# Attention and routed feed-forward on one Trainium2 core: the products with v in one piece for each half of the queries

## The chip, the cores and the metric

The kernel runs on one core of a Trainium2 chip. The metric is the device time of one execution in microseconds (us), from the launch to the end. Five engines work side by side, each through its own list of instructions in order: PE (TensorE: matrix products and transposes; the profile lists its weight loads apart, as PEld), DVE (VectorE), ACT (ScalarE), POOL (GpSimd) and SP (SyncE, which here only issues DMAs). PE writes into PSUM, which is divided into banks; DVE and ACT read PSUM and write the result to SBUF. An instruction that needs another engine's result waits on a semaphore, and everything behind it on its own engine waits too.

## The reference

Attention over 8 batches, 8 heads, 576 positions and head size 64, with a position bias from a small network, then a top-1 mixture of 8 experts over the 4608 tokens. Cut to what matters:

```python
scores = scale * np.matmul(q, k.transpose(0, 1, 3, 2))
scores = scores + bias.transpose(2, 0, 1)[None, :, :, :]
scores = scores - np.max(scores, axis=-1, keepdims=True)
attn = np.exp(scores)
attn = attn / (np.sum(attn, axis=-1, keepdims=True) + 1e-09)
attn_out = np.matmul(attn, v)
...
e_idx = np.argmax(logits, axis=1)
for e in range(E):
    mask = e_idx == e
    h = np.maximum(x[mask] @ w1[e], 0.0)
    out[mask] = gate_w[mask, None] * (h @ w2[e])
```

## The kernel before

Three stages follow each other: a table of the position bias, the attention (with the routing of finished batches spread through it), and the expert tiles. The change lies in the attention, `attention()` at L584. It runs over 32 pairs of heads (8 batches of 4 pairs) and one more turn that finishes the last pair. A turn n has five units u = 0 to 4. What a unit does, and in which order, is a string of letters in the table `ORDER` (L576 to L582); `attention()` walks through the letters and emits the instructions of each step. No scheduler moves anything afterwards, so the order of the letters is the order on every engine.

The letters that matter here:

- `S` is `scores()` (L415): the products of q and k for one slot (128 queries of one head; nine slots a pair, numbered S0 to S8 in this text, the last with six products instead of four) on PE into the PSUM tile `sps0` or `sps1`, then one DVE operation (L445) that adds the bias and finds the minimum (the score is kept negated).
- `e` and `f` are `exps()` (L457): the exponential of the unit's first and second slot on ACT.
- `T` and `t` are `etrans()` (L466) for part 1 and part 0: four transposes of a block of the exponentials on PE, into the PSUM tile `eps1` or `eps0`, and a copy into `eT` on ACT or DVE. The blocks are numbered by query chunk and part: e31 is chunk 3 part 1. Units 2, 3 and 4 do chunks 0, 1 and 2 of the turn's own pair; units 0 and 1 do chunks 3 and 4 of the pair before. Chunk 4 has only 64 queries for each head; its part 0 is e40 (L479, in `t` of unit 1), and its part 1 is the narrow one, e41 (L484, in `T` of unit 1), written into 64 columns of the array at a time.
- `R` is `rtrans()` (L495): four transposes of the last 64 keys of each row, copied into `rT` by ACT.
- `a A` and `b c` are `av()` (L504) of the pair before: the products of v and `eT`. Each half of the queries (288) takes eight of them, four key chunks for two heads, each in 64 columns of the array (L517), and one 128-wide product with the last 64 keys (L527), all summed in one PSUM bank. In the kernel before, a half comes in two pieces: `a` and `b` do key chunks 0 and 1, `A` and `c` do chunks 2 and 3, the 128-wide product, and the copy to `xT` on ACT (called av0 and av1).
- digits are `prep()` (L368): transposes of q and k of the next pair. `X` and `B` are steps of the routing, where there are any. `W`, `K`, `V`, `L` issue DMAs from SP; `C`, `q`, `k` are copies on POOL.

The PSUM banks `xps0` and `xps1` are handed out in turn by `xbank()` (L306): to `R`, the digits, `av()` and `X`. Which engine copies a block out of PSUM stands in `ON_ACT` (L310):

```python
ON_ACT = ("av0", "av1", "e00", "e11", "e20", "e30", "e31", "e40", "e41", "prep2", "prep5", "rT", "xr")
```

So e31, e30 and e40 are all copied by ACT, in this order, and e30 and e40 go through the same PSUM tile, `eps0`.

Of the kernel before, what the change touches and what calls it, by code (L numbers as in the profile page):

```python
# [22 lines left out]
S = 576  # L23
D = 64
# [4 lines left out]
HS = S // 2  # L29
# [78 lines left out]
class Attn:  # L108
# [392 lines left out]
            nc.tensor.transpose(ps[:, P * c : P * c + P], rem.rearrange("p h w -> p (h w)"), self.idf)  # L501
        self.take("rT", self.rT[:, 0:512], ps)

    def av(self, n, half, part):  # L504

        nc = self.nc
        if half == 0 and part == 0:
            self.xT[n] = self.xTb[n // NP % 2][:, n % NP, :]
        if part == 0:
            self.avps = self.xbank()  # L510
        v = self.vmain[n]
        sl = slice(HS * half, HS * half + HS)
        ps = self.avps[:, 0:HS]
        for k in (0, 1) if part == 0 else (2, 3):
            for h in range(2):
                o = slice(64 * h, 64 * h + 64)
                nc.tensor.matmul(  # L517
                    ps[o, :],
                    v[:, h, k, :],
                    self.eT[:, h, k, sl],  # L520
                    start=k == 0,
                    stop=False,
                    tile_position=(0, 64 * h),
                    skip_group_check=True,
                )
        if part == 1:
            nc.tensor.matmul(ps, self.vrem[n % 2], self.rT[:, sl], start=False, stop=True, skip_group_check=True)  # L527
        if part == 1:
            self.take(f"av{half}", self.xT[n][:, sl], ps)
            if half == 1:  # L530
                del self.vmain[n]

    def first_steps(self, route):

# [39 lines left out]


    ORDER = (  # L576
# [5 lines left out]
    )  # L582

    def attention(self):  # L584
        n_pair = self.n_pair
        tail = self.first_tiles() if self.K else {}
        for at in self.ROUTE_LATE:
            tail.setdefault(at, []).append(lambda: next(self.route, None))
        for u, k in self.LATE:
            tail.setdefault((0, u), []).append(lambda k=k: next(self.late[k], None))  # L590
        bg = None
        for n in range(n_pair + 1):
            for u in range(5):
                for f in tail.get((n, u), ()):
                    f()
                if u == 4 and n > 0 and n % NP == 0:
                    assert not bg or all(k == len(x) for x, k in bg)
                    bg = self.route_steps(n // NP - 1)
                m, w = (n, u - 2) if u >= 2 else (n - 1, u + 3)
                scored = []  # L600
                for op in self.ORDER[u].split():
                    if op in "SefC":
                        if n == n_pair:
                            continue
                        if op == "S":
                            scored.append(self.scores(n, 2 * u + len(scored)))
                        elif op == "C":
                            self.compact(n, u)
                        else:
                            self.exps(*scored["ef".index(op)])  # L610
                    elif op in "tT":
                        if 0 <= m < n_pair:
                            self.etrans(m, w, "tT".index(op))
                    elif op in "RaAbc":
                        if n > 0:
                            self.rtrans(n - 1) if op == "R" else self.av(n - 1, *divmod("aAbc".index(op), 2))
                    elif op in "01234WKV":
                        if n + 1 < n_pair:
                            if op in "01234":
                                self.prep(n + 1, int(op))()  # L620
                            else:
                                {"W": lambda: self.swap(n + 1), "K": lambda: self.heads(n + 1), "V": lambda: self.load_v(n + 1)}[op]()
                    elif op in "qkL":
                        if n + 2 < n_pair:
                            self.load_qk(n + 2) if op == "L" else self.split(n + 2, "qk".index(op))
                    elif op == "D":
                        self.route_store()
                    elif op == "Z":
                        self.route_scatter()
                    elif f := self.route_next(bg, "XB".index(op)):  # L630
                        f()
                if 0 <= m < n_pair:
                    del self.E[m, w]
        while self.scatters:
            self.route_scatter()
        self.bg = bg
# [836 lines left out]
```

## Time and profile before

| | |
|---|---|
| median of 3 runs | 1158.28 us (1153.8 to 1158.3) |
| the profiled execution's own time | 1160.33 us |
| its span, first to last instruction | 1158.4 us |
| mean granted TensorE clock | 0.99 of full speed |
| DVE, ACT, POOL busy, of the span | 65%, 63%, 31% |
| one pair in the middle of the attention, transposes of `R` to those of the next | 18.5 to 19.1 us |
| attention, first to last product with v | 86 to 679 us |

The profile is a trace of one execution. A row of the timeline gives the start in us, the length, the engine, the line of the kernel, the operation, what it writes and reads, the shape, how many instructions are merged into the row and, in brackets, how long the engine stood idle before it and what ended that. Each source-level product in full precision shows as two or more instructions, and a PE row overlaps the next by the depth of the array, so distances between starts are the safer measure. In all, 1024 instructions belong to L517 and 128 to L527.

### The profile page before, as it was taken

Reading aid. Unit: us, or ns where it says so; the run is one execution under the profiler, and the core shown is the slowest. Engines: PE = TensorE matmul, PEld = TensorE weight load, DVE = VectorE, ACT = ScalarE, POOL = GpSimd, SP = SyncE. Lnnn points to the kernel's source line nnn. Section 1 sums busy time; section 2 is a strip of 40 time slices with the busy share of each in tenths; the row PEclk is TensorE's granted clock in tenths of the full one; section 3 lists DMA queues with packets and bytes.
Section 4 is the critical chain, followed back from the end, with each engine's and each line's share of the span. In section 5 each row is a group of like instructions: output and inputs, shape, how many; then the busy total and the mean of one; then the engine's idle time right before and its main releaser. Section 6 shows DMA issues by size and latency. Waiting matters only on the chain. (4 is left out here: it accounts for less than half of the span.)

```text
span 1158.4 us, 23054 instructions
## 1 busy us (share of the span) xinstructions
PE 1121.5 (97%) x8202; PEld 912.4 (79%) x8202; DVE 748.6 (65%) x1556; ACT 731.8 (63%) x1420; POOL 361.0 (31%) x514
## 2 busy tenths in 40 slices
PE   7989999999999999999999999999999999999997
PEld 3457877778777777877777769899999999999975
DVE  8965667676675766756668547584566455645576
ACT  7776767767676676776766646454555455545576
POOL 0013334435434444254352234412112222212122
PEclk9989999999999999999999989999999999999999
DMA  6984434635545544454463721211115115112370
GB/s 176 222 173 113 107 97 124 115 96 130 110 108 121 123 122 104 105 129 108 121 121 96 204 33 56 60 47 46 56 38 175 62 57 196 42 47 65 110 261 26
DMA packets 91456, 124.54 MB, mean 108 GB/s; under 512 B 35713, under 2 KB 60673, under 8 KB 91332
## 3 DMA queue, kind: packets, MB, share of 16 engines
q1 hardware_dynamic: 83236, 101.61, 34.8%
q0 software_dynamic: 8000, 21.35, 6.2%
q8 instruction: 68, 1.11, 0.5%
q14 instruction: 56, 0.46, 0.2%
q10 hardware_dynamic: 96, 0.00, 0.0%
HBM read 140.36 MB, written 19.90 MB: 138 GB/s over the span
## 5 line engine op out<-in xcount | busy, mean ns | idle before, releaser
L445 DVE CUSTOM_DVE_ANT_0 Eb<-sps,NBm 128x576 f32<-128x576 f32 x256 | 189.6, 754 | 160.0 <-PE sps L430 89.1
L459 ACT ACTIVATE Eb<-Eb,mn 128x576 f32<-128x576 f32 x288 | 221.4, 769 | 36.9 <-DVE mn L445 33.5
L430 PE MATMUL sps<-KT,QT 128*128 128x288 f32 x1152 | 220.4, 317 | 3.9 <-DMA QT<-QT 3.7
L430 PEld LDWEIGHTS sps<-KT,QT 128*128 128x128 f32 x1152 | 164.6, 190 | 9.0 <-issue 4.5
L1188 PE MATMUL p<-QT,w1hi 128*128 128x256 f32 x1152 | 162.2, 284 | 0.0
L473 PE MATMUL eps<-idf,Eb 128*128 128x128 f32 x1024 | 158.5, 281 | 0.6 <-DVE lgs L810 0.3
L517 PE MATMUL xps<-eT,vraw 128*64 128x288 f32 x1024 | 155.1, 425 | 1.5 <-DVE QT L1173 1.0
L1188 PEld LDWEIGHTS p<-QT,w1hi 128*128 128x128 f32 x1152 | 149.5, 192 | 2.2 <-ACT w1hi L1161 0.8
L473 PEld LDWEIGHTS eps<-idf,Eb 128*128 128x128 f32 x1024 | 113.9, 141 | 39.0 <-issue 29.3
L1191 DVE SCALAR_TENSOR_TENSOR hl<-p,hh 128x512 fp32r<-128x512 f32 x72 | 49.7, 690 | 141.5 <-ACT hh L1190 140.0
L1214 POOL DMA_INDIRECT out<-mo,idt x36 | 48.0, 1333 | 298.5 <-ACT mo L1213 262.4
L464 POOL COPY rem<-Eb 128x128 f32<-128x128 f32 x128 | 37.2, 291 | 318.8 <-ACT Eb L459 312.3
L1155 DVE TENSOR_TENSOR w2lo<-NBm,w2hi 128x1024 fp32r<-128x1024 f32 x84 | 102.3, 1224 | 24.8 <-ACT w2hi L1154 18.7
L1205 PE MATMUL p<-w2hi,hh 128*128 128x512 f32 x288 | 115.3, 400 | 0.0
L315 ACT ACTIVATE eT<-eps 128x512 f32<-128x512 f32 x192 | 110.6, 591 | 6.8 <-PE eps L473 5.9
L1205 PE MATMUL p<-w2hi,hl 128*128 128x512 f32 x288 | 113.7, 395 | 0.0
L1190 ACT ACTIVATE hh<-p 128x512 fp32r<-128x512 f32 x72 | 43.0, 597 | 111.5 <-PE p L1188 101.3
L315 ACT ACTIVATE xTb<-xps 128x288 f32<-128x288 f32 x64 | 26.3, 411 | 117.0 <-PE xps L527 114.4
L517 PEld LDWEIGHTS xps<-eT,vraw 128*64 128x64 f32 x1024 | 63.2, 138 | 46.1 <-issue 12.3
L1155 DVE TENSOR_TENSOR w1lo<-NBm,w1hi 128x1024 fp32r<-128x1024 f32 x84 | 97.7, 1225 | 0.2 <-ACT w1hi L1154 0.2
L1188 PE MATMUL p<-QT,w1lo 128*128 128x256 f32 x576 | 92.9, 284 | 1.0 <-DVE w1lo L1162 1.0
L1154 ACT CAST w2hi<-NBm 128x1024 fp32r<-128x1024 f32 x84 | 86.8, 1040 | 0.7 <-PEq L1318 0.7
(235 smaller groups left out, 1945.9 us busy)
## 6 DMA issues: line engine op xcount, KB each, us to landing
NBm<-moe_w SPq DMA_DIRECT2D x24, 2048.0 KB
NBm<-moe_w SPq DMA_DIRECT2D x46, 1024.0 KB
QT<-QT SPq DMA_DIRECT2D x64, 304.0 KB
NBm<-xTb SPq DMA_DIRECT2D x32, 288.0 KB
KH<-KT SPq DMA_DIRECT2D x64, 144.0 KB
qraw<-q SPq DMA_DIRECT2D x32, 256.0 KB
kraw<-k SPq DMA_DIRECT2D x32, 256.0 KB
vraw<-v SPq DMA_DIRECT2D x32, 256.0 KB
```

The costliest lines, as they stand in the source:

```text
L315: self.nc.scalar.activation(out, ps, AF.Copy, scale=scale)
L430: nc.tensor.matmul(ps[:, half, :], q, k[:, HS * half : HS * half + HS], start=i == 0, stop=i == len(terms) - 1, skip_group_check=True,)
L445: nc.vector.tensor_tensor_reduce(out=e.rearrange("p (t w) -> p t w", t=2), in0=ps, in1=nb.rearrange("p (t w) -> p t w", t=2), scale=1.0, s ...
L459: self.nc.scalar.activation(e, e, AF.Exp, bias=mn, scale=-1.0, accum_out=sm)
L473: nc.tensor.transpose(ps[:, k, :], e[:, part, P * k : P * k + P], self.idf)
L517: nc.tensor.matmul(ps[o, :], v[:, h, k, :], self.eT[:, h, k, sl], start=k == 0, stop=False, tile_position=(0, 64 * h), skip_group_check=True,)
L1154: self.nc.scalar.copy(h, w)
L1155: self.nc.vector.tensor_tensor(l, w, h.bitcast(F32), op=ALU.subtract)
L1188: nc.tensor.matmul(ps[:, a, :], w[:, c, fs], x[:, c, :], start=i == 0, stop=i == len(ops) - 1)
L1191: nc.vector.scalar_tensor_tensor(hl[:, sl, :], ps, 0.0, hh[:, sl, :].bitcast(F32), op0=ALU.max, op1=ALU.subtract)
L1205: nc.tensor.matmul(ps, h[:, f, sl], m[:, f, :], start=i == 0, stop=i == len(ops) - 1)
L1214: nc.gpsimd.indirect_dma_start(out=self.out, out_offset=IndirectOffsetOnAxis(ap=ids, axis=0), in_=o, in_offset=None, bounds_check=self.n_t ...
```

## The change

`av()` loses its argument `part`: one call does all eight products of a half, the 128-wide product and the copy. The table `ORDER` has one letter for each half instead of two. `a` (first half) stands in unit 1 behind `T`, the narrow transposes, instead of `a` in unit 0 and `A` in unit 1. `b` (second half) stands where it stood, in unit 2, and takes in what `c` did in unit 3. In unit 1 `T` moves up from the end to a place ahead of `a`, and `0` comes behind `a`; in unit 0 `t` directly follows `T`.

```diff
-    def av(self, n, half, part):
+    def av(self, n, half):
...
-        if part == 0:
-            self.avps = self.xbank()
...
-        ps = self.avps[:, 0:HS]
-        for k in (0, 1) if part == 0 else (2, 3):
+        ps = self.xbank()[:, 0:HS]
+        for k in range(4):
...
-        if part == 1:
-            nc.tensor.matmul(ps, self.vrem[n % 2], self.rT[:, sl], start=False, stop=True, skip_group_check=True)
-        if part == 1:
-            self.take(f"av{half}", self.xT[n][:, sl], ps)
-            if half == 1:
-                del self.vmain[n]
+        nc.tensor.matmul(ps, self.vrem[n % 2], self.rT[:, sl], start=False, stop=True, skip_group_check=True)
+        self.take(f"av{half}", self.xT[n][:, sl], ps)
+        if half == 1:
+            del self.vmain[n]
...
     ORDER = (
-        "S R S e f X T a t B C Z",
-        "L D S 1 A t e S 4 f 0 C T",
+        "S R S e f X T t B C Z",
+        "L D S 1 t e S 4 f T a 0 C",
         "t S W S e f b q C Z T",
-        "B S c e S T 3 2 t f C V",
+        "B S e S T 3 2 t f C V",
         "S K k X X e T B X t D",
     )
```

The lines of `av()` are L515 and L524 in the changed kernel. The first place is PE's list in units 0 and 1, from e31 (`eps1`) to e40 (L479 into `eps0`). Before, in turn 10:

```order
L473 MATMUL eps1_739<-idf_62,Eb_88 128x128 [waits DVE_49,Activation_49]
L473 MATMUL eps1_739<-idf_62,Eb_88 128x128 x3
L517 MATMUL xps1_78<-eT_103,vraw9_2588 64x288 [waits DMAHW7_49,Activation_49]
L517 MATMUL xps1_78<-eT_103,vraw9_2588 64x288 x3
L473 MATMUL eps0_738<-idf_62,Eb_88 128x128 x4
L430 MATMUL sps0_736<-KT0_107,QT0_72 128x288 [waits DVE_49]
L430 MATMUL sps0_736<-KT0_107,QT0_72 128x288 x3
L379 MATMUL xps0_77<-idr_102,qs_105 128x128 [waits Activation_49]
L379 MATMUL xps0_77<-idr_102,qs_105 128x128 x3
L517 MATMUL xps1_78<-eT_103,vraw9_2588 64x288 x4
L527 MATMUL xps1_78<-rT_104,vrem1_116 128x288 [waits DMAHW1_49,DMAHW0_49]
L479 MATMUL eps0_738<-idf_62,Eb_88 128x128 [waits Activation_49]
```

The same stretch of PE's list in the changed kernel, in the same turn, again from e31 to e40:

```order
L473 MATMUL eps1_739<-idf_62,Eb_88 128x128 [waits DVE_49,Activation_49]
L473 MATMUL eps1_739<-idf_62,Eb_88 128x128 x3
L473 MATMUL eps0_738<-idf_62,Eb_88 128x128 [waits Activation_49]
L473 MATMUL eps0_738<-idf_62,Eb_88 128x128 x3
L430 MATMUL sps0_736<-KT0_107,QT0_72 128x288 [waits DVE_49]
L430 MATMUL sps0_736<-KT0_107,QT0_72 128x288 x3
L379 MATMUL xps1_78<-idr_102,qs_105 128x128 x4
L479 MATMUL eps0_738<-idf_62,Eb_88 128x128 [waits Activation_49]
L479 MATMUL eps0_738<-idf_62,Eb_88 128x128 x3
```

Both pieces of the first half have left the stretch between e31 and e40; between the two uses of `eps0` there remain one group of scores and one of prep. In both kernels the first transpose of e40 waits on ACT.

The second place is PE's list from the second scores of unit 2 (`sps1`) to the second of unit 3, with the second half of the products with v. Before:

```order
L430 MATMUL sps1_737<-KT0_107,QT0_72 128x288 [waits DVE_49]
L430 MATMUL sps1_737<-KT0_107,QT0_72 128x288 x3
L517 MATMUL xps1_78<-eT_103,vraw9_2588 64x288 [waits Activation_49]
L517 MATMUL xps1_78<-eT_103,vraw9_2588 64x288 x3
L473 MATMUL eps1_739<-idf_62,Eb_88 128x128 [waits Activation_49]
L473 MATMUL eps1_739<-idf_62,Eb_88 128x128 x3
L430 MATMUL sps0_736<-KT0_107,QT0_72 128x288 [waits DVE_49]
L430 MATMUL sps0_736<-KT0_107,QT0_72 128x288 x3
L517 MATMUL xps1_78<-eT_103,vraw9_2588 64x288 x4
L527 MATMUL xps1_78<-rT_104,vrem1_116 128x288
L430 MATMUL sps1_737<-KT0_107,QT0_72 128x288 [waits DVE_49]
L430 MATMUL sps1_737<-KT0_107,QT0_72 128x288 x3
```

The changed kernel's PE list over the same stretch, which here begins with both scores of unit 2:

```order
L430 MATMUL sps0_736<-KT0_107,QT0_72 128x288 x4
L430 MATMUL sps1_737<-KT0_107,QT0_72 128x288 x4
L515 MATMUL xps1_78<-eT_103,vraw9_2588 64x288 [waits Activation_49]
L515 MATMUL xps1_78<-eT_103,vraw9_2588 64x288 x7
L524 MATMUL xps1_78<-rT_104,vrem1_116 128x288
L473 MATMUL eps1_739<-idf_62,Eb_88 128x128 x4
L430 MATMUL sps0_736<-KT0_107,QT0_72 128x288 [waits DVE_49]
L430 MATMUL sps0_736<-KT0_107,QT0_72 128x288 x3
L430 MATMUL sps1_737<-KT0_107,QT0_72 128x288 [waits DVE_49]
L430 MATMUL sps1_737<-KT0_107,QT0_72 128x288 x3
```

The eight products stand together, and the two groups of scores of unit 3 now follow each other with nothing between.

The third place is ACT's list in units 0 and 1: from the exponential of S1 (`mn10_1`) over the copies of e31 (`eps1`), e30 (`eps0`), av0 (`xTb`) and e40 (`eps0`) to the exponential of S2. Before:

```order
L459 ACTIVATE Eb_88,sums10_2852<-Eb_88,mn10_1_2864 128x576 [waits DVE_49,Activation_49]
L315 ACTIVATE eT_103<-eps1_739 128x4x128 [waits PE_49]
L315 ACTIVATE eT_103<-eps0_738 128x4x128 [waits PE_49]
L315 ACTIVATE xTb0_94<-xps1_78 128x288 [waits PE_49]
L315 ACTIVATE eT_103<-eps0_738 128x4x2x64 [waits PE_49]
L459 ACTIVATE Eb_88,sums10_2852<-Eb_88,mn10_2_2906 128x576 [waits DVE_49]
```

ACT's list in the changed kernel over the same stretch, continued to av0:

```order
L459 ACTIVATE Eb_88,sums10_2852<-Eb_88,mn10_1_2864 128x576 [waits DVE_49,Activation_49]
L315 ACTIVATE eT_103<-eps1_739 128x4x128 [waits PE_49]
L315 ACTIVATE eT_103<-eps0_738 128x4x128 [waits PE_49]
L315 ACTIVATE eT_103<-eps0_738 128x4x2x64 [waits PE_49]
L459 ACTIVATE Eb_88,sums10_2852<-Eb_88,mn10_2_2902 128x576 [waits DVE_49]
L315 ACTIVATE KT1_108<-xps0_77 128x2x64 [waits DMAHW4_49,DMAHW2_49,DVE_49]
L459 ACTIVATE Eb_88,sums10_2852<-Eb_88,mn10_3_2919 128x576 [waits Activation_49]
L315 ACTIVATE rT_104<-eps1_739 128x64 [waits PE_49]
L315 ACTIVATE xTb0_94<-xps1_78 128x288 [waits PE_49]
```

On ACT only av0 has moved, behind the copy of e41 (`rT`); the copies of e31 and e30 still stand behind the exponential of S1.

More of the change, by code (lines that the diff above doesn't have):

```diff
@@ L502, in rtrans @@
         self.take("rT", self.rT[:, 0:512], ps)
-    def av(self, n, half, part):
+    def av(self, n, half):
         nc = self.nc
-        if half == 0 and part == 0:
+        if half == 0:
             self.xT[n] = self.xTb[n // NP % 2][:, n % NP, :]
-        if part == 0:
-            self.avps = self.xbank()
         v = self.vmain[n]
         sl = slice(HS * half, HS * half + HS)
-        ps = self.avps[:, 0:HS]
-        for k in (0, 1) if part == 0 else (2, 3):
+        ps = self.xbank()[:, 0:HS]
+        for k in range(4):
             for h in range(2):
@@ L613, in attention @@
                             self.etrans(m, w, "tT".index(op))
-                    elif op in "RaAbc":
+                    elif op in "Rab":
                         if n > 0:
-                            self.rtrans(n - 1) if op == "R" else self.av(n - 1, *divmod("aAbc".index(op), 2))
+                            self.rtrans(n - 1) if op == "R" else self.av(n - 1, "ab".index(op))
                     elif op in "01234WKV":
```

## The prediction

> **What bounds the kernel now.** I read the page first, then the waits of PE in the middle of the attention (200 to 588 us), then the timeline of single pairs. The page says who is busy:
>
> ```profile
> PE 1121.5 (97%) x8202; PEld 912.4 (79%) x8202; DVE 748.6 (65%) x1556; ACT 731.8 (63%) x1420; POOL 361.0 (31%) x514
> ```
>
> PE is busy 97% of the span, and no other engine passes 65%. An average can hide stages, so the waits of PE inside the attention come next (who waited for whom, us in total, times, longest):
>
> ```profile
> PE xps L866 <- DVE base L847: 1.5, 5, 0.3
> PE xps L771 <- DVE xrb L317: 1.1, 3, 0.4
> PE sps L430 <- DMA QT<-QT: 0.4, 1, 0.4
> ```
>
> That is the whole list: 3.0 us in 388. PE is the bound there, and each microsecond taken from or added to its list moves the end by as much. That holds only as long as the other engines deliver in time, and how near they are must be read from the order. Units 0 and 1 of a turn, on PE, from e31 (514.03) by `a`, e30, S2, prep 1, `A` and its 128-wide product to e40 (L479):
>
> ```profile
> 514.03 0.60 PE L473 MATMUL eps<-idf,Eb 128*128 128x128 f32 x4
> 514.56 1.19 PE L517 MATMUL xps<-eT,vraw 128*64 128x288 f32 x8
> 515.68 0.66 PE L473 MATMUL eps<-idf,Eb 128*128 128x128 f32 x4
> 516.09 0.78 PE L430 MATMUL sps<-KT,QT 128*128 128x288 f32 x4
> 516.71 0.45 PE L379 MATMUL xps<-idr,qs 128*128 128x128 f32 x4
> 517.09 1.19 PE L517 MATMUL xps<-eT,vraw 128*64 128x288 f32 x8
> 518.21 0.75 PE L527 MATMUL xps<-rT,vrem 128*128 128x288 f32 x2
> 518.80 0.60 PE L479 MATMUL eps<-idf,Eb 128*128 128x128 f32 x4
> ```
>
> ACT at the same time: the exponential of S1, then the copies of e31 and e30 in one row of two, with no idle time in brackets:
>
> ```profile
> 515.09 0.78 ACT L459 ACTIVATE Eb<-Eb,mn 128x576 f32<-128x576 f32 x1
> ...
> 515.86 1.11 ACT L315 ACTIVATE eT<-eps 128x512 f32<-128x512 f32 x2
> ```
>
> The copy of e30 ends at 515.86 + 1.11 = 516.97. e40 needs the same PSUM tile and starts at 518.80, 1.83 us later. So ACT, though busy 63%, is only 1.83 us ahead here, and what keeps it ahead is PE's work on `a` and `A`.
>
> **The change: what PE saves.** Every entry into the 64-column products and every way out of them costs PE time. The way out, in the weight loads:
>
> ```profile
> 515.68 0.42 PEld L473 LDWEIGHTS eps<-idf,Eb 128*128 128x128 f32 x4 [0.44 <-issue]
> ```
>
> The next weights are not loaded beside the running products, as elsewhere, but 0.44 us later. To price whole pieces I use distances between starts, with these rows of units 1 to 4 of the pair before:
>
> ```profile
> 501.51 0.22 PE L384 MATMUL xps<-idr,qs 128*128 128x128 f32 x1
> ...
> 502.07 0.34 PE L484 MATMUL eps<-idf,Eb 128*64 128x64 f32 x4
> 502.33 0.66 PE L473 MATMUL eps<-idf,Eb 128*128 128x128 f32 x4
> 502.74 1.30 PE L430 MATMUL sps<-KT,QT 128*128 128x288 f32 x8
> 503.98 1.19 PE L517 MATMUL xps<-eT,vraw 128*64 128x288 f32 x8
> 505.10 0.66 PE L473 MATMUL eps<-idf,Eb 128*128 128x128 f32 x4
> 505.51 0.78 PE L430 MATMUL sps<-KT,QT 128*128 128x288 f32 x4
> ...
> 508.46 0.60 PE L473 MATMUL eps<-idf,Eb 128*128 128x128 f32 x4
> 508.81 0.88 PE L379 MATMUL xps<-idr,ks 128*128 128x128 f32 x8
> 509.53 0.63 PE L473 MATMUL eps<-idf,Eb 128*128 128x128 f32 x4
> ...
> 511.66 1.04 PE L473 MATMUL eps<-idf,Eb 128*128 128x128 f32 x8
> ```
>
> - Unit prices. Four transposes ahead of another group take 0.35 (508.46 to 508.81), and ahead of more transposes 0.44 (eight in 1.04, the last of them about 0.27 long, so 0.11 each). Four of prep take 0.36 (eight from 508.81 to 509.53). A piece of four products with v and the way out takes 1.12 (503.98 to 505.10). Its row of 1.19 has four steps of two concurrent products; a product is 0.41 long, so a step is at most 0.26, and the first is slower, so I take 0.245. Eight products then take 1.12 + 4 x 0.245 = 2.10. The 128-wide product takes 0.59 (518.21 to 518.80).
> - Units 0 and 1, e31 to e40: 518.80 - 514.03 = 4.77 before. Left are e31 0.44, e30 0.35, S2 0.62 (516.09 to 516.71) and prep 1 0.36, together 1.77. PE's list is shorter by **3.00**.
> - Unit 3: from S6 (505.51) to e11 (508.46) 2.95. Two groups of scores take 1.24 up to a product with v (502.74 to 503.98), and 0.09 of that is the entry (514.03 to 514.56 is 0.53 where four transposes take 0.44), so 1.15 is left: shorter by **1.80**.
> - Unit 1, from prep 4 to S4: 501.51 to 502.74 is 1.23 before, with prep 0. Now prep 4 0.20, the narrow transposes 0.26 (502.07 to 502.33), eight products 2.10, the 128-wide one 0.59, prep 0 0.36, e00 0.35, together 3.86: longer by **2.63**.
> - Unit 2, `b` and the transposes behind it: 503.98 to 505.51 is 1.53; now 2.10 + 0.59 + 0.35 = 3.04: longer by **1.51**.
>
> The sum is -3.00 - 1.80 + 2.63 + 1.51 = -0.66, say 0.7 us a pair, 32 x 0.7 = **22 us** less work in PE's list. DVE, ACT, POOL and the DMAs have as many instructions as before.
>
> **The change: what PE now waits for.** The 3.00 us that leave units 0 and 1 were the cover of ACT. The copy of e30 cannot come sooner: it stands behind the exponential of S1, which needs DVE's operation on S1, which needs S1 on PE, and none of these moved ahead. So e40 reaches PE's head 3.00 us sooner against a copy that had 1.83 us in hand: a wait of 3.00 - 1.83 = 1.17 us. This pair is the good end. The bad end is a pair whose routing steps delay DVE, two pairs later:
>
> ```profile
> 554.18 1.05 ACT L315 ACTIVATE eT<-eps 128x512 f32<-128x512 f32 x2
> ...
> 556.30 0.49 PE L479 MATMUL eps<-idf,Eb 128*128 128x128 f32 x3
> ```
>
> Here the hand is 556.30 - 555.23 = 1.07, the wait 1.93. With the middle, 1.55, over the 31 turns that have both a pair before and scores of their own: **48 us**. Behind e40 on PE stand S3, prep 4, the narrow transposes, `a` and prep 0; DVE and ACT wait for these in turn, with no work to fill the time.
>
> Smaller places. SP passes nothing new, but prep 0 comes later behind `a`, so the swap `W` is issued later; it is first needed by S0 of the next turn, some 8 us on, and PE's waits on that transfer were 0.4 us in all. `a` takes its bank from prep 1, whose DVE copy stands before DVE's operation on S3; with PE held at e40 that copy is early. In unit 3 S6 and S7 now come back to back, so DVE's copy of e01 and its operations on S6 and S7 queue:
>
> ```profile
> 506.47 0.75 DVE L445 CUSTOM_DVE_ANT_0 Eb<-sps,NBm 128x576 f32<-128x576 f32 x1
> ...
> 508.66 0.76 DVE L445 CUSTOM_DVE_ANT_0 Eb<-sps,NBm 128x576 f32<-128x576 f32 x1 [1.43 <-PE sps L430]
> ```
>
> They stood 2.19 us apart. ACT's chain from there to e30 (exponentials of S6, S7, S8, S0, S1 with the copies between) can fall behind PE by between nothing (it had idle time in the stretch) and about 0.4 us; I take 0.15, **5 us** in all, and keep 0 and 12 for the range.
>
> **The clock.** A longer idle time of PE can cost more than itself. Windows of the trace (length, PE busy, PEclk, DMA):
>
> ```profile
> 664.73:668.14 3.41, 1.66 (x12) 1.00 0.01 0
> 668.14:674.97 6.83, 6.23 (x25) 0.50 0.73 88
> 1108.35:1111.77 3.42, 2.25 (x10) 1.00 0.43 146
> ```
>
> After 3.41 us with 1.66 busy (1.75 idle) the granted clock is 0.50; a window with 1.17 idle (1108.35), which holds a wait as long as the good end here, drew nothing: the mean clock of the whole span is 0.99. The waits of 1.2 to 1.9 us straddle that boundary. Where one falls whole into such a window, 3.41 us at half clock cost another 1.7 us. I count half of the 8 pairs at the bad end: 4 x 1.7 = **7 us**.
>
> The Trainium skill (TensorE: Matmul & The Clock Gate, "Why this matters for your kernels") says that only idle gaps of over about 3 us between bursts bring the clock down. By that rule no wait here would, and the sum would be 7 us less. The trace does not agree: the row above shows half clock behind 1.75 us of idle time.
>
> **The sum.** On the profiled execution's own 1160.3 us (its span is 1158.4): 1160.3 - 22 + 48 + 5 + 7 = 1198. That execution lies 2 us above the median of the runs, 1158.3, so 1196.
>
> **Rivals.**
> - *The saving comes alone* (8%): the copy of e30 is no bound, and PE has 22 us less to do: 1136. For it speaks that ACT and DVE are idle over a third of the time. It decides where the copy of e30 ends within 1.77 us of e31's start, or the wait stays under 0.7 us; in the rows it ends 516.97 - 514.03 = 2.94 after it.
> - The Trainium skill (TensorEngine Tiling (Array Packing), "Key Properties") has a rule for this side: a change of the tiling mode drains TensorE, so fewer changes are faster. The 0.44 us row agrees; by that rule alone the time would be this rival's.
> - *Half the wait is hidden* (6%): 31 x 0.75 = 23 against 22, no change, 1158 to 1175. It needs ACT to run ahead by 0.8 us at S1, against which its rows without idle time speak.
> - *The clock falls in most pairs* (20%): 16 to 24 windows at half clock cost 27 to 41 us instead of 7: 1210 to 1230. Against it: the window with 1.17 idle.
> - *The forecast* (66%): 1180 to 1210.
>
> The range 1176 to 1218 takes in the forecast, the lower part of the clock's case and both ends of the small terms. A measurement of this kernel can tell about 0.5% from no change. Faster by more than that 7%, within it 5%, slower 88%.
>
> **What would show it.** Right: in the waits, PE at e40 (L479) held by ACT's copy to `eT` (L315), some 48 us in 31 waits; pairs of some 19.5 to 20 us where they were 18.5 to 19.1; half as many 0.44 us waits of PEld around the products with v; PEclk under 1.00 in single windows. Wrong: no wait at L479, or one on DVE at the scores of unit 4 (L430), which would mean that I mis-sized the queue behind e01.

## The result and the profile after

The changed kernel takes 1199.59 us (median of 4 runs, 1198.54 to 1201.94), the kernel before 1158.01 us (median of 4, 1153.8 to 1158.3) in the same session. The ratio is 1.0371, 95% interval 1.0342 to 1.0399: **slower**, near the predicted 1196 and inside its range. The profiled execution took 1201.94 us (span 1200.1), 41.6 us more than that of before, at a mean clock of 0.979 instead of 0.990.

From the page of the changed kernel, who is busy:

```profile
PE 1117.8 (93%) x8202; PEld 925.7 (77%) x8202; DVE 747.9 (62%) x1556; ACT 733.6 (61%) x1420; POOL 363.3 (30%) x514
```

PE is busy 3.7 us less in the sum, although half the clock is granted more often; and it is idle 7% of the span instead of 3%. The waits of PE from 100 to 700 us (total us, times, longest):

```profile
PE eps L479 <- ACT eT L315: 43.7, 30, 3.1
PE sps L430 <- DVE mn L445: 4.5, 9, 1.3
```

The list of before had 3.0 us; now e40 alone waits 43.7 us for ACT's copies. The weight loads around the products with v show what the merging saved. PEld's waits, first before (100 to 665 us; L517 and L527 are the products with v), then after (100 to 700 us; now L515 and L524):

```profile
PEld eps L473 <- issue: 27.3, 65, 0.4
PEld xps L527 <- issue: 21.0, 48, 0.4
```

```profile
PEld eps L479 <- ACT eT L315: 48.0, 30, 3.3
PEld xps L524 <- issue: 24.4, 55, 0.7
...
PEld eps L473 <- issue: 1.5, 6, 0.3
```

The ways out of the 64-column products straight into transposes (L473) went from 27.3 to 1.5 us; those into the 128-wide product, which the change keeps, stayed.

Turns are not alike. Once batches are being routed, n%4 decides which routing steps stand in a turn. Four turns in a row from the middle of the attention, n%4 = 0, 1, 2, 3 (length; busy us and instructions of PE, PEld, DVE, ACT, POOL; PEclk, DMA share, GB/s), first before, then after:

```profile
513.06:531.59 18.53, 18.53 (x147) 14.03 (x145) 11.61 (x26) 13.06 (x33) 9.78 (x15) 1.00 0.61 124
531.59:550.34 18.75, 18.40 (x152) 14.58 (x150) 12.31 (x34) 12.26 (x31) 6.14 (x14) 1.00 0.39 98
550.34:569.45 19.11, 18.78 (x148) 14.77 (x147) 15.12 (x47) 13.95 (x35) 6.33 (x11) 1.00 0.41 103
569.45:588.41 18.96, 18.95 (x150) 15.22 (x149) 10.85 (x25) 13.68 (x32) 9.93 (x16) 1.00 0.59 136
```

```profile
547.18:566.13 18.95, 17.86 (x147) 14.09 (x146) 11.49 (x31) 13.21 (x33) 9.70 (x15) 1.00 0.66 120
566.13:584.45 18.32, 17.63 (x151) 14.61 (x150) 11.41 (x29) 12.44 (x31) 6.17 (x13) 1.00 0.41 100
584.45:607.06 22.61, 20.35 (x149) 16.15 (x148) 15.39 (x47) 13.82 (x35) 6.29 (x10) 0.92 0.34 86
607.06:629.77 22.71, 19.58 (x151) 16.32 (x149) 11.24 (x26) 13.77 (x32) 10.19 (x17) 0.92 0.41 115
```

The first two turns changed by +0.42 and -0.43 us, the last two by +3.50 and +3.75, and only these have PEclk under 1.00. The last one is the longest of its kind in the changed kernel; the other five turns with n%4 = 3 in the routed part take 21.9 to 22.4 us.

**The wait itself**, in the first of these turns. PE's timeline from e31 to S3, and ACT's at the same time:

```profile
548.15 1.03 PE L473 MATMUL eps<-idf,Eb 128*128 128x128 f32 x8
548.94 0.78 PE L430 MATMUL sps<-KT,QT 128*128 128x288 f32 x4
549.55 0.46 PE L379 MATMUL xps<-idr,qs 128*128 128x128 f32 x4
551.10 0.66 PE L479 MATMUL eps<-idf,Eb 128*128 128x128 f32 x4 [1.09 <-ACT eT L315]
```

```profile
549.98 1.06 ACT L315 ACTIVATE eT<-eps 128x512 f32<-128x512 f32 x2
```

The copies of e31 and e30 end at 549.98 + 1.06 = 551.04, and e40 starts at 551.10. PE had nothing left to do from 550.01 on.

**The wait in turns with n%4 = 2.** PE's rows of S2 and e40, and DVE's rows of a routing step and of its operation on S0:

```profile
587.14 0.80 PE L430 MATMUL sps<-KT,QT 128*128 128x288 f32 x4 [0.46 <-DVE mn L445]
...
589.77 1.10 PE L479 MATMUL eps<-idf,Eb 128*128 128x128 f32 x4 [1.53 <-ACT eT L315]
```

```profile
585.39 0.55 DVE L806 TENSOR_TENSOR lgs<-lgs,mbias 128x40 f32<-128x40 f32 x1
...
586.32 0.76 DVE L445 CUSTOM_DVE_ANT_0 Eb<-sps,NBm 128x576 f32<-128x576 f32 x1
```

S2 needs the PSUM tile of S0, whose operation ends at 587.08 because routing steps stand ahead of it. So PE waits twice, 1.99 us in all.

The same turns have a third wait, in unit 4, which the list of PE's waits above does not show, because it stands in the weight loads. The weights of S8, after and then before:

```profile
603.26 0.56 PEld L430 LDWEIGHTS sps<-KT,QT 128*128 128x128 f32 x4 [0.33 <-DVE mn L445]
```

```profile
565.65 0.56 PEld L430 LDWEIGHTS sps<-KT,QT 128*128 128x128 f32 x4
```

S8 uses the PSUM tile of S7, and DVE is late with S7: the copy of e01, three routing steps and the operation on S6 stand ahead of it. This is the queue behind back-to-back scores for which the prediction set 5 us.

**The wait in turns with n%4 = 3.** PE's e40, and ACT ahead of it:

```profile
367.33 0.66 PE L479 MATMUL eps<-idf,Eb 128*128 128x128 f32 x4 [2.74 <-ACT eT L315]
```

```profile
365.70 0.60 ACT L315 ACTIVATE xrb<-xps 128x512 f32<-128x512 f32 x1 [1.40 <-DMA xg<-xrb]
366.19 1.08 ACT L315 ACTIVATE eT<-eps 128x512 f32<-128x512 f32 x2
```

Here ACT itself waits 1.40 us: the routing's copy to `xrb` (step `X`) needs a buffer whose rows are still being stored, and e31 and e30 queue behind it. In the six turns of this kind the same copy waited 0.3 to 0.7 us for these rows in the kernel before, and 1.0 to 1.8 in the changed kernel. This row no step of the prediction had.

**The clock.** Two windows behind each other, twice (length, PE busy and instructions, PEclk, DMA share, GB/s):

```profile
422.57:425.98 3.41, 1.67 (x14) 1.00 0.61 166
425.98:429.39 3.41, 3.16 (x18) 0.50 0.03 7
651.26:654.67 3.41, 1.98 (x16) 1.00 0.40 104
654.67:658.08 3.41, 2.03 (x20) 1.00 0.25 76
```

Here 1.74 us of idle time in a window is followed by one at half clock, and 1.43 us is not. From 100 to 665 us the changed kernel has 12 windows at half clock, the kernel before none (it has two from 668 us on, which the changed kernel has not). They come in pairs, one in a turn with n%4 = 2 and one in the turn behind it, at 180 and 204 us, 262 and 286, 344 and 368, and so on to 590 and 614: every 82 us, which is 24 windows and also the length of four turns.

### The profile page after: what moved, and what is told of

It is laid out like the page before. It is cut to its first block, busy times and chain, and to the rows that moved or that the text cites. A ratio compares the mean times of both kernels' runs of the same rounds, so it can differ in the third digit from the quotient of the medians.

```text
span 1200.1 us, 23067 instructions
## 1 busy us (share of the span) xinstructions
PE 1117.8 (93%) x8202; PEld 925.7 (77%) x8202; DVE 747.9 (62%) x1556; ACT 733.6 (61%) x1420; POOL 363.3 (30%) x514
## 5 line engine op out<-in xcount | busy, mean ns | idle before, releaser
L445 DVE CUSTOM_DVE_ANT_0 Eb<-sps,NBm 128x576 f32<-128x576 f32 x256 | 186.9, 753 | 86.4 <-PE sps L430 41.2
L430 PE MATMUL sps<-KT,QT 128*128 128x288 f32 x1152 | 213.6, 317 | 9.1 <-DVE mn L445 4.7
L473 PE MATMUL eps<-idf,Eb 128*128 128x128 f32 x1024 | 148.5, 276 | 0.6 <-ACT rT L315 0.4
L515 PE MATMUL xps<-eT,vraw 128*64 128x288 f32 x1024 | 147.2, 433 | 0.0
L473 PEld LDWEIGHTS eps<-idf,Eb 128*128 128x128 f32 x1024 | 114.5, 141 | 14.5 <-DVE mn L445 5.0
L317 DVE COPY eT<-eps 128x512 f32<-128x512 f32 x96 | 66.2, 689 | 71.9 <-ACT xTb L315 67.7
L515 PEld LDWEIGHTS xps<-eT,vraw 128*64 128x64 f32 x1024 | 72.7, 147 | 49.4 <-issue 15.4
L319 DVE TENSOR_SCALAR QT<-xps 128x512 fp32r<-128x512 f32 (+1 forms) x96 | 53.2, 555 | 84.0 <-PE xps L379 83.7
```

Of the source, the lines that this page charges most:

```text
L317: self.nc.vector.tensor_copy(out, ps)
L319: self.nc.vector.tensor_scalar(out, ps, scale, None, op0=ALU.mult)
L430: nc.tensor.matmul(ps[:, half, :], q, k[:, HS * half : HS * half + HS], start=i == 0, stop=i == len(terms) - 1, skip_group_check=True,)
L445: nc.vector.tensor_tensor_reduce(out=e.rearrange("p (t w) -> p t w", t=2), in0=ps, in1=nb.rearrange("p (t w) -> p t w", t=2), scale=1.0, s ...
L473: nc.tensor.transpose(ps[:, k, :], e[:, part, P * k : P * k + P], self.idf)
L515: nc.tensor.matmul(ps[o, :], v[:, h, k, :], self.eT[:, h, k, sl], start=k == 0, stop=False, tile_position=(0, 64 * h), skip_group_check=True,)
```

## The experiments

Each ran beside the kernel before on the same chip; ratios are against that. Edits are against the changed kernel unless said otherwise. Lengths of turns (from the transposes of `R` to the next, in the profiled execution) where they matter, the usual value of each kind:

| kernel | ratio (95%) | early turn, no routing | n%4 = 0 | 1 | 2 | 3 |
|---|---|---|---|---|---|---|
| before | 1 | 17.38 | 18.53 | 18.75 | 19.11 | 18.7 to 19.0 |
| the change | 1.0371 (1.0342 to 1.0399) | 17.98 | 18.95 | 18.32 | 22.61 | 21.9 to 22.7 |
| e1 | 1.0053 (1.0036 to 1.007) | 16.82 | 17.95 | 17.75 | 19.62 | 19.6 to 20.0 |
| e2 | 1.0106 (1.0075 to 1.0136) | 16.73 | 17.88 | 17.67 | 21.6 | 18.65 |
| e5 | 1.0026 (1.0004 to 1.0048) | 17.11 | 18.24 | 18.06 | 19.2 | 19.1 |
| e6 | 1.0315 (1.0276 to 1.0354) | 18.25 | 19.20 | 19.49 | 20.6 | 19.9 to 22.6 |
| e7 | 0.9985 (0.9962 to 1.0008) | 17.22 | 18.36 | 18.17 | 19.31 | 18.52 |
| e8 | 1.0018 (1.0 to 1.0037) | 17.46 | 18.61 | 18.82 | 19.19 | 18.76 |
| e12 | 0.9966 (0.9946 to 0.9985) | | 17.94 | 17.74 | 19.31 | 18.52 |

### The cover given back: e1

```diff
-        "L D S 1 t e S 4 f T a 0 C",
+        "L D S 1 a t e S 4 f T 0 C",
```

> The change, but the first half's eight products and their 128-wide one stand ahead of e40 in unit 1 (order 'L D S 1 a t e S 4 f T 0 C'), so PE has work while ACT copies e30. Wait theory: no wait at L479, no window at half clock in the attention, and what is left is the saving of two pieces' entries and ways out, about 0.55 us a pair: 1140 us (1132 to 1150). Rival, the long pieces themselves are the cost (eight products in a row starve DVE and ACT): still slower than before, 1170 us or more.

1160.51 against 1155.24 us. No wait at L479 is left, and the early turns are 0.56 us shorter than before: the merging saves what was forecast, and the loss was the wait. But turns with n%4 = 2 and 3 are longer than before by some 0.5 to 1.2 us. Its waits of PE from 84 to 720 us, and two turns (n%4 = 1, then 2):

```profile
PE xps L515 <- ACT xrb L315: 9.2, 6, 1.8
PE sps L430 <- DVE mn L445: 4.5, 9, 1.3
PE sps L430 <- DMA QT<-QT: 3.4, 1, 3.4
```

```profile
307.70:325.40 17.70, 17.70 (x151) 14.67 (x150) 11.34 (x29) 12.30 (x31) 6.03 (x13) 1.00 0.46 104
325.40:345.00 19.60, 18.89 (x148) 15.02 (x146) 15.28 (x47) 13.70 (x35) 6.17 (x10) 1.00 0.39 98
```

The same two late things remain, only at other places: `a` waits for the bank that the copy to `xrb` frees, and S2 waits for DVE. Unit 0 lost its piece `a` in this kernel too. S8's weights wait as in the change. In the profiled execution a late swap of `QT` costs 3.4 us besides, and two windows at half clock follow it. So the expected 1132 to 1150 was missed.

### The copy taken from ACT: e2

```diff
-    ON_ACT = (..., "e20", "e30", "e31", ...)
+    ON_ACT = (..., "e20", "e31", ...)
```

> The change with its order as it is, only the copy of e30 goes to DVE, which is idle there, instead of ACT, where it stands behind the exponential of S1. Wait theory: the waits at L479 fall from 44 us to under 6, the windows at half clock go, and the saving of 0.7 to 0.8 us a pair shows: 1136 us (1130 to 1148). Rival, the long pieces are the cost: nothing on PE has moved, so 1190 us or more.

1167.91 against 1155.24 us. The wait at L479 is 1.6 us in all, so it was ACT's copy of e30. The time did not come down to before, since turns with n%4 = 2 have a new wait:

```profile
PE xps L515 <- DVE QT L319: 12.0, 8, 1.7
PE sps L430 <- DMA QT<-QT: 6.6, 3, 3.3
```

`a` takes the bank of prep 1, whose copy is DVE's; with e30 taken to DVE as well, that copy stands behind routing steps on five lines. The expected 1130 to 1148 was missed by this and by the late swaps.

### The tile changed: e3

```diff
-            ps = self.eps[0]
+            ps = self.eps[1]
```

(in e40's branch; e41 goes to `eps[0]` in exchange)

> The change, but e40 goes through eps1 and e41 through eps0, so e40 waits for the copy of e31, which ACT ends 0.5 us before that of e30. Wait theory: each of some 30 waits is 0.5 us shorter (44 to about 29 us in all), the windows at half clock become fewer, and each that goes gives 1.7 us: 1164 to 1182 us. Rival, the long pieces are the cost: within 5 us of the change, 1195 to 1204.

1178.87 against 1155.24 us, ratio 1.0215 (1.0196 to 1.0233), and the wait is just the size expected:

```profile
PE eps L479 <- ACT eT L315: 28.9, 30, 2.4
```

One copy less to wait for takes 0.5 us from each wait, and half the windows at half clock go with it (6 are left).

### The idle time filled: e4

```diff
-            for j in range(4):
+            for j in (0, 1, 2, 3) * (3 if part == 1 and n > 1 else 1):
```

The transposes of prep 1 run three times from the second pair on, with the same values.

> The change, with the four transposes of prep 1 done three times over from the second pair on (the same values into the same bank), 0.72 us more work on PE just ahead of e40. The wait at L479 is fixed by ACT, so it shrinks by what is added and e40 starts when it did. If the windows at half clock cost time of their own (1.7 us each): they become few, and the time falls although PE does 23 us more work: 1176 to 1187 us. If they cost nothing or come from something other than PE's idle time: 1198 to 1206 us.

1192.25 against 1155.24 us, ratio 1.0312 (1.0278 to 1.0347). The extra transposes stand in the idle time and shorten the recorded wait, but e40 starts no sooner: turns with n%4 = 0 and 1 take 18.94 and 18.34 us, as in the change. Its wait:

```profile
PE eps L479 <- ACT eT L315: 23.5, 23, 3.0
```

PE does more work and the kernel is faster than the change, by little: the two intervals of the ratio touch. Its own four executions go with their mean clock: 1188.04 us at 0.990, 1189.64 at 0.988, 1194.85 and 1196.09 at 0.984. So the clock has a price. The price itself, from two turns of this kernel with n%4 = 2, one without and one with a window at half clock:

```profile
337.80:358.80 21.00, 19.42 (x155) 15.59 (x154) 15.47 (x47) 13.78 (x35) 6.23 (x10) 1.00 0.35 91
497.30:520.00 22.70, 21.14 (x157) 16.84 (x156) 15.60 (x47) 13.90 (x35) 6.30 (x10) 0.92 0.35 85
```

1.70 us each. Seven windows are left of 12; 5 x 1.7 = 8.5 us, and the ratio fell by 0.0059, 7 us. Neither expected time was met, because the filler broke not all windows but fewer than half.

### Each half alone: e5 and e6

e5 leaves the first half as before (`a` in unit 0, `A` in unit 1) and does the second in one piece in unit 2; e6 does the first in one piece where the change has it and leaves the second as before (`b` in unit 2, `c` in unit 3).

Both are edits of the kernel before, in which `av()` gets an argument for a whole half; `g` is the whole first half and `h` the whole second.

```diff
 e5:
-        "t S W S e f b q C Z T",
-        "B S c e S T 3 2 t f C V",
+        "t S W S e f h q C Z T",
+        "B S e S T 3 2 t f C V",
 e6:
-        "S R S e f X T a t B C Z",
-        "L D S 1 A t e S 4 f 0 C T",
+        "S R S e f X T t B C Z",
+        "L D S 1 t e S 4 f T g 0 C",
```

> The kernel before with one part of the change: the second half in one piece at the end of unit 2, the first half in two pieces as before. The cover of e30's copy is untouched. Theory: no wait at L479, no windows at half clock, and about 0.3 us a pair saved by one entry and one way out less, of which up to 5 us go to the queue in unit 3 where S6 and S7 now meet: 1143 to 1153 us, wait of PE at S8 (L430 on DVE) under 0.2 us each. Rival, the long piece and the queue behind it cost more than the entry: 1158 us or more.

> The other part alone: the first half in one piece behind the narrow transposes in unit 1, the second half in two pieces as before. Theory: all of the loss sits here: waits at L479 of 38 to 46 us and the windows at half clock as in the change, 1195 to 1210 us. Rival, half of the loss comes from the second half: 1172 to 1185 us.

e6: 1193.07 against 1154.15 us, ratio 1.0315 (1.0276 to 1.0354), with nearly the whole wait:

```profile
PE eps L479 <- ACT eT L315: 41.4, 29, 2.7
```

So most of the loss sits in the move of the first half. The time is 2 us under the expected 1195 to 1210: the wait is in its range of 38 to 46, but from 100 to 665 us e6 has 6 windows at half clock, where the change has 12. Taken without its wait of 1.29, an early turn saves 0.41 us.

e5: 1158.2 against 1154.15 us. Early turns are 0.27 us shorter, but no time comes of it. In the profiled execution the turns with n%4 = 2 and 3 are mostly 0.1 to 0.4 us longer than before, and four turns are 1.1 to 3.3 us longer (20.5, 22.1, 20.2, 19.6 us); its waits of PE list 3.7 us for the swap of `QT` and 5.1 us for the copy to `xrb`, where the kernel before has 1.3 us each. Why the copy to `xrb` is later stays open. The expected 1143 to 1153 was missed, and so was the small wait at S8: its weights wait for DVE by 0.32 to 0.50 us in nine turns.

### The first half between e31 and e30: e7 and e8

e7 puts the whole first half where its first piece stood before. e8 moves the second half into unit 3 besides, between S6 and S7.

```diff
+e7, e8:    "S R S e f X T a t B C Z",
+e7, e8:    "L D S 1 t e S 4 f 0 C T",
...
+e8:        "t S W S e f q C Z T",
+e8:        "B S e b S T 3 2 t f C V",
```

> Both halves in one piece, the second as in the change, the first in unit 0 between e31 and e30 where the first of the two pieces stood before (order 'S R S e f X T a t B C Z', 'L D S 1 t e S 4 f 0 C T'). Then 2.9 us of PE's work stand between the exponential of S1's input and e30, and S2, prep 1 and e40 come later for the routing pairs too. Theory: the waits on e30's copy, on the bank behind the stored rows and on S0's DVE operation are all covered, and the saving of 0.55 to 0.6 us a pair shows: 1136 to 1146 us. Rival, a wait in the routing pairs takes the saving as in the run with the first half ahead of e40: 1153 to 1163 us.

> As the run with the first half between e31 and e30, and the second half in one piece too, but in unit 3 between S6 and S7 (order 't S W S e f q C Z T', 'B S e b S T 3 2 t f C V'). If the queue of DVE and ACT behind S6 and S7 costs (0.15 us a pair and more in routing pairs), it goes: 2 to 8 us faster than that run. If it costs nothing: within 3 us of it, or slower if e01 or S6 now come late.

e7: 1153.57 against 1154.15 us, no difference that can be told. The wait at L479 is gone (0.8 us) and with it every regular wait of this list:

```profile
PE sps L430 <- DMA QT<-QT: 5.7, 4, 2.7
...
PE eps L479 <- ACT eT L315: 0.8, 4, 0.3
```

What is left are single late swaps of `QT`. Its turns are 0.2 to 0.6 us shorter than before except with n%4 = 2, and the expected 1136 to 1146 was missed. Early turns gain 0.16 where those of e1 gain 0.56. Most of that difference stands in the weight loads: prep 0 takes the bank of prep 1 and waits for DVE's copy of it, 0.27 us in an early turn (waits of PEld, 100 to 662 us):

```profile
PEld xps L379 <- DVE QT L319: 6.8, 26, 0.3
```

e8: 1157.99 against 1154.15 us, 4.4 us slower than e7. With S6 and S7 apart the turns are longer than in e7 by 0.24 to 0.65 us in three kinds of four. Most of the 0.24 is again a lost cover: with the second half gone from unit 2, S6 comes sooner, and its weights wait 0.22 us for DVE in every turn, the late S6 that the expectation named. In the fourth kind, n%4 = 2, e8 is shorter by 0.12: there S8's weights wait 0.33 us for DVE in e7 and not in e8, and from the transposes ahead of S8 to the end of the turn e8 takes 4.17 us, e7 4.53 and the kernel before 4.16. So the queue behind back-to-back scores costs some 0.37 us in these turns and nothing that shows in the early ones.

### Covers and the routing step: e9, e10, e11

Three kernels move the routing step `X` from unit 0 behind other work in unit 1, to take the waiting copy to `xrb` out of ACT's way: e9 with the first half early in unit 1, e10 alone on the kernel before, e11 alone on the change. Their output is not the reference's: by the order of the steps, with `X` behind `D`, the rows of one query chunk in each batch are overwritten in their buffer before they are stored.

```diff
+e9:     "S R S e f T t B C Z",
+e9:     "L D a S 1 X t e S 4 f T 0 C",
+e10:    "S R S e f T a t B C Z",
+e10:    "L D S 1 A X t e S 4 f 0 C T",
+e11:    "S R S e f T t B C Z",
+e11:    "L D S 1 X t e S 4 f T a 0 C",
```

> Both halves in one piece, with the first half straight behind e30 and ahead of S2, and unit 0's routing step X moved into unit 1 behind prep 1 (order 'S R S e f T t B C Z', 'L D a S 1 X t e S 4 f T 0 C', the rest as in the change). PE's 2.9 us then stand ahead of S2, whose DVE operation is late in one routing pair, and ahead of e40; and ACT copies e31 and e30 before it waits for the stored rows in the other. Theory (three late things need the cover, the copy of e30 in every pair, S0's DVE operation and the stored rows in one pair of four each): 0.4 to 0.55 us a pair saved, 1137 to 1147 us. Rival, the routing pairs wait elsewhere: 1150 to 1160 us.

> The kernel before with unit 0's routing step X moved into unit 1 behind the first half's second piece, and nothing else. Theory: in the kernel before everything is covered, so nothing is gained: 1150 to 1158 us. Rival, the step's place is worth time by itself: 1148 us or less, and then it has to be taken off what the run before this one gains.

> The change with unit 0's routing step X moved into unit 1 behind prep 1 (order 'S R S e f T t B C Z', 'L D S 1 X t e S 4 f T a 0 C'). Theory: in the pairs where X copies rows, ACT no longer waits 1.4 us for stored rows ahead of the copies of e31 and e30, and PE has X as work: the waits at L479 there fall from 2.3 to 2.7 us to 1.2 or less, their windows at half clock go (half of the 13), and the time falls by 18 to 28 us: 1171 to 1182 us. Rival, the wait in these pairs comes from ACT being behind already when unit 0 begins: 1190 us or more.

e9: 1168.96 us, ratio 1.0115 (1.0048 to 1.0183). e10: 1170.92 us, 1.014 (1.0106 to 1.0173), slower by the move alone. e11: 1198.57 us, 1.0374 (1.0339 to 1.041), against 1154.04 us each. All three expectations of the time were missed; e11 lies where its rival put it, at 1190 or more. In its turns with n%4 = 3 the wait at e40 fell from 2.3 to 3.1 us to 1.03. But in the same turns PE now waits 1.07 to 1.31 us for ACT at e30 (L473) as well, so ACT is still late there, as the rival has it. Its waits from 84 to 720 us:

```profile
PE eps L479 <- ACT eT L315: 22.2, 21, 1.3
PE eps L473 <- ACT eT L315: 6.7, 6, 1.3
PE sps L430 <- DMA QT<-QT: 6.0, 2, 3.2
```

That the copy to `xrb` stands waiting ahead of the two copies is shown by the trace of the change; what the change would cost without that is not shown.

### The place chosen by the kind of turn: e12

The first half as in e7 for n%4 = 2 and 3, as in e1 for 0 and 1; the second in one piece as in the change.

```diff
+    def order(self, n, u):
+
+        if n % NP in (2, 3):
+            return {0: "S R S e f X T a t B C Z", 1: "L D S 1 t e S 4 f 0 C T"}.get(u, self.ORDER[u])
+        return {1: "L D S 1 a t e S 4 f T 0 C"}.get(u, self.ORDER[u])
...
-                for op in self.ORDER[u].split():
+                for op in self.order(n, u).split():
```

> Both halves in one piece, the second as in the change; the first half ahead of e40 in unit 1 in the two turns of four that the run with that order made shorter (turns 0 and 1 of a batch), and between e31 and e30 in unit 0 in the two turns with late DVE work and stored rows (2 and 3). Theory (the saving is there, and what eats it in a turn depends on what is late in that turn): the four turns take 17.95, 17.75, 19.3 and 18.5 us as in the two runs apart, 73.5 against 75.2 before, so 13 us over 32 pairs less 0 to 6 us for later transfers of q: 1140 to 1148 us, faster than the kernel before by more than its interval. Rival, what one turn saves the next one waits for: within 0.4% of the kernel before.

1151.26 us (1144.29 to 1157.75) against 1155.71: ratio 0.9966 (0.9946 to 0.9985). It beats both kernels, by 0.3% and about 4%, but the expected 1140 to 1148 was missed, and the gain is no more than the rival allowed. The usual turns are as the parts gave; single turns are not. In turn 8 (22.3 us) S0 waits for the swap of `QT`; PE's row, then SP's rows of the two swaps here and in the kernel before:

```profile
PE sps L430 <- DMA QT<-QT: 7.6, 4, 3.9
```

```profile
221.59 0.54 SPq L403 DMA_DIRECT2D QT<-QT  x1
225.48 0.48 SPq L404 DMA_DIRECT2D QT<-QT  x1
```

```profile
221.28 0.54 SPq L403 DMA_DIRECT2D QT<-QT  x1
221.87 0.59 SPq L404 DMA_DIRECT2D QT<-QT  x1
```

SP issues the second swap 3.9 us after the first instead of 0.6. The trace puts 3.3 us of that down to a DMA of the routing's rows; why it comes so late in single turns stays open. Two windows at half clock follow the wait, and turn 9 takes 20.15 us. The execution with the highest mean clock, 0.997 where the others have 0.989 to 0.993, is also the fastest, 1144.29 us.

## Why the prediction was right

- **The bound.** Right: what PE waited for moved the end.
- **What PE saves** (22 us). Right in the early turns, and some 3 us too much over all. Early turns without routing went from 17.38 to 17.98 with a wait of 1.29, so 16.69 without it: 0.69 us a turn where 0.66 was worked out. e5 and e6 show the two parts, 0.27 and 0.41. In turns with n%4 = 2 next to nothing is saved: PE is busy 18.89 us in e1 and 18.78 before. The rule of the Trainium skill (TensorEngine Tiling (Array Packing), "Key Properties") that changing the tiling mode drains TensorE is borne out in its direction by these numbers; it was outweighed.
- **What PE waits for** (48 us). Right in place, cause and sum: 44.6 us in 31 waits over the whole attention. e1 and e2 took the wait away, each by another way, and e3 shortened it by the length of a copy; e6 put it on the first half. The sizes by turn were not 1.17 to 1.93: they were 1.29 in the early turns and then 1.09, 0.69, 1.53 and 2.3 to 3.1 for n%4 = 0 to 3. The pair taken for the good end had n%4 = 0, 1.09 where 1.17 was worked out. The pair taken for the bad end had n%4 = 2, where part of the delay shows earlier, at S2: 1.99 in all where 1.93 was worked out. The worst pairs were the next ones, through the copy to `xrb`, whose wait for stored rows was 0.3 to 0.7 us before. The middle came out because the errors went both ways.
- **The queue behind e01** (5 us). Right in place, too large, and partly hidden. S8's weights wait 0.32 to 0.49 us for DVE in nine turns of the changed kernel, in no early one. They do the same in e1, e5, e7 and e12, where S6 and S7 also come back to back, and in e6 and e8, where they stand apart, only once, by 0.22 us, as in the kernel before. At the 0.37 us that e7 and e8 differ by, nine turns make some 3 us. The prediction's sign of a mis-sized queue, a wait on DVE at the scores of unit 4, is this one. The 4.5 us in 9 waits of PE on DVE at the scores are mostly another thing: eight of them are at S2 behind routing steps, uncovered by the loss of `a` in unit 0, which the prediction had not counted.
- **The clock** (7 us). The mechanism was right and the term was mis-sized: 12 windows instead of 4, at 1.70 us, 20 us, less 3 us for the two windows at 668 us that are gone. The step that failed is "half of the 8 pairs at the bad end": the waits of two kinds of turn are long enough, and the batch settled on a length of 24 windows, so that in each batch the same two waits fall whole into a window. The Trainium skill (TensorE: Matmul & The Clock Gate, "Why this matters for your kernels") puts the gap to avoid at over about 3 us; here waits of 1.5 to 3.1 us were enough, 1.74 us idle in a window the least.
- **The sum.** The forecast adds 38 us to the profiled execution of before, and 41.6 were measured. From the first transposes of `R` to the last, 582.5 us became 629.3. PE's idle time there grew from 7.5 to 53.2, which is 45.7: the waits at e40 and on DVE, less the smaller waits of before that fell away. PE's busy time grew by 1.1, although 39.9 us more at half clock are worth some 20; so its work fell by some 19. Ahead of and behind that stretch 5.2 us were gained, where before has more windows at half clock. That the sum came so near is in part luck: the clock cost 13 us more than forecast and the saving was 3 us smaller, and the idle time, 7 us under the forecast, and these 5 us made up for most of it.
- **The rivals.** The saving alone and half the wait hidden are out. The case of a falling clock in most pairs was nearer in its windows (12, where it began at 16) than the forecast was (4). By the prediction's own terms 12 windows give 1209 and 16 give 1216, not the 1210 that it names. The time fell into the forecast's range for the reasons given under the sum.
- **The signs.** Pairs of 19.5 to 20 us held for no kind of turn: two stayed at 18.3 to 19.0, two went to 21.9 to 22.7, 20.5 in the mean. The weight loads' waits around the products with v fell as named, from 113 to 61 (L473 and the 128-wide product together, lists above), and the single windows under 1.00 came.

## What to carry to other kernels

Before work is taken from between two uses of one PSUM tile, read how long the copy between them ends ahead of its reader, in each kind of turn and not in one: that distance is what may be taken, here 1.83 us of 3.00. Look at the weight loads as well as at the products: waits of 0.2 to 0.3 us in nearly every turn stood there in e7 and e8. The same piece of work can be the cover for several things at once (here e30's copy in every turn, DVE behind routing steps in one of four, ACT behind a DMA in another), and a fix for one shows the next. A merging that saves 0.7 us is best put where the order still leaves cover, which can differ by turn, as e12 shows.

## What the runs showed of the hardware beside that

- The windows of the clock are a grid of 3.41 us. A loop with idle time in it can lock to that grid: from 180 to 614 us six batches in a row have two windows at half clock each, at the same places, 82 us or 24 windows apart.
- What decides is the idle time within one window of the grid and not the length of a wait. In e3, waits of 1.84 to 1.98 us in five turns with n%4 = 3 were each followed by a window at half clock, while the longest, 2.38 us up to 357.03 us, was not. The early turns of the change, each with a wait of some 1.29 us, have no window at half clock.
- The profile's busy time gives no sharp bound for it. In the traces of all fourteen kernels, from 84 us on, every window of the grid with PE busy under 1.57 us was followed by half clock, and of those at full clock none with over 2.16. Between the two both occur: in the changed kernel 1.67 us of busy time at 422.57 us drew it, and 1.67 us at 1190.57 us did not.
- From the end of ACT's copy to the start of the waiting product on PE went 0.05 to 0.06 us in the turns read; the handover itself is a small part of the loss.
